# A Fourier mixing layer and a SoLU layer on one core: sorting the late units' transposed tokens by sign, and moving two products one step later

## The chip, the cores and the metric

The kernel runs on 1 core of one Trainium2 chip. The metric is the device time of one execution in microseconds (us), the median of several executions. The engines that matter here are TensorE (matrix products, "PE" in the profile, with its weight loads on a row of their own, "PEld"), VectorE ("DVE"), ScalarE ("ACT"), GpSimd ("POOL") and SyncE, which issues most DMAs ("SP"). Each engine works through its own instructions in program order and waits on the others through semaphores.

## The reference

```python
# x: (8, 3136, 256); w_in: (256, 1024); w_out: (1024, 256); g_ln: (1024,)
X = np.fft.fft(x, axis=1)
X = np.fft.fft(X, axis=2)
x = X.real.reshape(25088, 256)
h = x @ w_in
e = np.exp(h - max(h))                  # over the 1024 features of a token
solu = h * e / (sum(e) + 1e-9)
ln = (solu - mean(solu)) / sqrt(var(solu) + 1e-6) * g_ln
out = ln @ w_out                        # (25088, 256), float32
```

## The kernel before

The transform over the 3136 tokens of a sequence is split as 49 x 64. `transform1` makes the first part for a pair of sequences, chunk by chunk, and keeps it in DRAM (`zd`); `transform2` makes the second part for one frequency. The symmetry of a real input lets one result `q` serve two rows of the output, called the two signs; the transform over the features is folded into `w_in`. Four pairs of sequences give 100 units (25 of each pair), each of 128 tokens of either sign; the first unit of each pair (units 0, 25, 50, 75) has one sign only. A unit goes through `up` (the product with `w_in`), `even`, `join`, `expo`, `product`, `square` (SoLU and its statistics), is transposed by 32 x 32 blocks on VectorE (`turn_blocks`), has its blocks moved across partitions by DMA (`move_blocks`, once for two units, 16 DMAs), and four steps later meets `w_out`. There, odd units with both signs use the seven products of a Strassen-like scheme (`Down`, `sums`, `product7`), spread over an odd step and the following even one; the other units use two plain products (`down`), the first in an even step, the second (`plain`) in the following odd one.

In the transposed tile `uT` the tokens of the two signs alternate: the last index of `v` is the sign. The main loop works at step `i` on unit `i`, on the last products of unit `i - 4`, and on the first transform of the next pair (`ahead`, `ahead_pe`). `result(0)` is one PSUM bank, which `transform2`, `transform1` of the later pairs and the second plain product share.

```python
    qpool = ctx.enter_context(tc.tile_pool(name="qpool", bufs=4))
    ...
    def result(i):
        return ps_m.tile([P, 2 * D], FP32, tag=f"m{i % 4}", name="ps_m")
    ...
    def transform1(pr, s):
        ...
        ps = result(0 if pr.p else s).rearrange("p (l d) -> p l d", l=2)
        if s == NH // 2 - 1:
            parts = [(ps[0:ZR, 0], y[:, l], 0), (ps[0:ZR, 1], pr.y0[:, 0], 1), (ps[0:ZR, 1], y[:, l + 1], 2)]
        else:
            parts = [(ps[0:ZR], y[:, l : l + 2], 0)]
        pr.done.append(s)
        first = True
        for o, i, t in parts:
            for h, cs in enumerate((EVEN, ODD)):
                nc.tensor.matmul(o[..., cs], F[:, 2 * t + h, :], i[..., cs], start=first, stop=True,
                                 skip_group_check=True)
                first = False
        nc.scalar.copy(pr.z[:, l : l + 2, :], ps[0:ZR])
        if l == CH - 2:
            keep(pr, c, slice(0, ZR if pr.p else 4 * KG))
    ...
    def transform2(pr, k1):
        i, k = divmod(k1, KG)
        g = pr.g[i]
        table = T[0][:, :, k, :] if i == 0 else T[1][:, :, k1 - KG, :]
        ps = result(0)[:, 0 : KD * P]
        for h in range(KD):
            o = ps[:, h * P : (h + 1) * P].rearrange("p (b k) -> p b k", b=2)
            nc.tensor.matmul(o, g[:, k, h * P : (h + 1) * P], table,
                             start=(h == 0), stop=True, skip_group_check=True)
        return ps
    def take2(t, ps):
        t.q = qpool.tile([P, KD * P], FP32, tag="q", name="q")
        nc.scalar.copy(t.q, ps)
    def spread(t):
        t.r = small.tile([P, 1], FP32, tag="r", name="r")
        nc.sync.dma_start(out=t.r, in_=t.q[0:1, P : 2 * P])
    ...
    def up(t, c):
        ps = ps_h.tile([P, FF], FP32, tag=f"h{c}", name=f"ps_h{c}")
        for half in range(2):
            fs = slice(half * HW, (half + 1) * HW)
            nc.tensor.matmul(ps[:, fs], t.q[:, c * P : (c + 1) * P], Wi[:, c, fs], start=True, stop=True)
        return ps
    def even(t, ps):
        t.ev = fpool.tile([P, FF], FP32, tag="ev", name="ev", bufs=1)
        nc.vector.scalar_tensor_tensor(out=t.ev, in0=w_mid, scalar=t.r, in1=ps,
                                       op0=ALU.mult, op1=ALU.add)
    def join(t, s):
        if s == 0:
            t.nmax = small.tile([P, 2], FP32, tag="nmax", name="nmax")
        t.h[s] = fpool.tile([P, FF], FP32, tag="h", name="h", bufs=2)
        nc.vector.tensor_tensor_reduce(out=t.h[s], in0=t.h[0] if s else t.ev, in1=t.odd, scale=1.0 if s else -0.5,
                                       scalar=-3.0e38, op0=ALU.add, op1=ALU.max, accum_out=t.nmax[:, s : s + 1])
    ...
    class Batch:
        def __init__(self, by_blocks):
            if by_blocks:
                self.v = fpool.tile([P, 2, FF, 2], FP32, tag="v", name="v32", bufs=2)
            self.uT = fpool.tile([P, 2, KF, 4, 64], FP32, tag="uT", name="uT", bufs=2)
    def turn_blocks(t, s):
        for o in (s,) if len(t.signs) == 2 else (0, 1):
            nc.vector.transpose(out=t.batch.v[:, t.w, :, o], in_=t.u[s])
    ...
    def move_blocks(batch, units, engines=(nc.sync,)):
        v = batch.v[:, units].rearrange("p w (c q n) s -> p q (w c) (n s)", q=4, n=32)
        uT = batch.uT[:, units].rearrange("p w c i m -> p i (w c) m")
        for i in range(4):
            for q in range(4):
                a, b = slice(32 * i, 32 * i + 32), slice(32 * q, 32 * q + 32)
                engines[i % len(engines)].dma_start(out=uT[b, i], in_=v[a, q])
    ...
    def blocks(t):
        uT = t.batch.uT[:, t.w].rearrange("p c i (n s) -> p s c (i n)", s=2)
        return [uT[:, s, c : c + KF // 2] for s in range(2) for c in (0, KF // 2)]
    def sums(t):
        A11, A12, A21, A22 = blocks(t)
        t.S = spool.tile([P, 4, KF // 2, P], FP32, tag="S", name="S")
        for j, (a, b, op) in enumerate(((A21, A22, ALU.add), (t.S[:, 0], A11, ALU.subtract),
                                        (A11, A21, ALU.subtract), (A12, t.S[:, 1], ALU.subtract))):
            nc.gpsimd.tensor_tensor(out=t.S[:, j], in0=a, in1=b, op=op)
    def product7(o, a, b, start=False):
        n = KF // 2
        for c in range(n):
            nc.tensor.matmul(o, a[:, c], b[:, c], start=start and c == 0, stop=c == n - 1, skip_group_check=True)
    ...
    # class Down: seven products of a unit with both signs; the four quarters of the result are sums of them
        def p1(self):
            product7(self.C11, self.A11, Wo[:, 0 : KF // 2, 0:P], True)
        def seed(self):
            nc.scalar.copy(self.X, self.C11)
        def p4(self):
            product7(self.P53, self.A22, Ws[:, 3], True)
        def keep4(self):
            self.keep(1, 0, self.P53)
        def p2(self):
            product7(self.C11, self.A12, Wo[:, KF // 2 :, 0:P])
        def keep11(self):
            self.keep(0, 0, self.C11)
        def p5(self):
            product7(self.P53, self.t.S[:, 0], Ws[:, 0], True)
        def p6(self):
            product7(self.X, self.t.S[:, 1], Ws[:, 1])
        def p3(self):
            product7(self.P53, self.t.S[:, 3], Wo[:, KF // 2 :, P:])
        def p7(self):
            product7(self.X, self.t.S[:, 2], Ws[:, 2])
    ...
    def down(t, s, ps=None):
        uT = t.batch.uT[:, t.w].rearrange("p c i (n s) -> p c (i n) s", s=2)
        if ps is None:
            ps = (result(0) if s else bank(0))[:, 0:D]
        for c in range(KF):
            nc.tensor.matmul(ps, uT[:, c, :, s], Wo[:, c, :], start=(c == 0), stop=(c == KF - 1))
        return ps
    ...
    SUMS = [None] + [[f + 2 * c for c in range(NC)] for f in (3, 27, 51)]
    ...
    def ahead_pe(pr, i, half):
        for c in range(NC):
            if i == SUMS[pr.p][c] + 3:
                transform1(pr, c * CH // 2 + half)
    ...
        for i in range(whole + 1, len(units) + lag + 3):
            cur = units[i] if i < len(units) else None
            old = units[i - lag] if i < len(units) + lag else None
            seven = old and by_seven(i - lag)
            plain, late, scaled = late, None, []
            kept = units[i - lag - 3] if i > whole + 2 else None
            if seven:
                sums(old)
            if fresh:
                power(fresh)
            fresh = cur
            if kept:
                for s in kept.signs:
                    store(kept, s)
            if done:
                done.finish()
                done = None
            if cur:
                enter(i)
                even(cur, up(cur, 0))
                cur.odd = up(cur, 1)
                second_transform(i + 2)
                for s in cur.signs:
                    join(cur, s)
            if seven:
                new = Down(old, i == whole + 1)
                new.p1()
                new.seed()
            if half:
                half.p5()
                half.keep5()
                half.p6()
            if cur:
                expo(cur, 0)
            if half:
                half.keep6()
            if cur:
                if 1 in cur.signs:
                    expo(cur, 1)
                other_pairs(i, ahead_pe, 0)
            if plain:
                ps_o = down(*plain)
                if not cur:
                    scale(*plain, ps_o)
                    plain = None
            if seven:
                new.p4()
                new.p2()
            elif old is units[-1]:
                for s in (1, 0):
                    scaled.append((old, s, down(old, s, bank(2 * s)[:, 0:D])))
            elif old:
                scaled.append((old, 0, down(old, 0)))
                late = (old, 1) if 1 in old.signs else None
            if half:
                half.p3()
                half.p7()
                half, done = None, half
            if cur:
                for s in cur.signs:
                    product(cur, s)
                square(cur, 0)
            if plain:
                scale(*plain, ps_o)
            if seven:
                new.keep4()
                new.keep11()
                half = new
            if cur:
                if 1 in cur.signs:
                    square(cur, 1)
                other_pairs(i, ahead_pe, 1)
                for s in cur.signs:
                    turn_blocks(cur, s)
                if i >= len(units) - 2:
                    move_blocks(batches[-1], slice(cur.w, cur.w + 1), (nc.sync, nc.gpsimd) if cur.w else (nc.sync,))
                elif cur.w:
                    move_blocks(batches[-1], slice(0, 2))
                stats(cur)
            for t, s, ps_o in scaled:
                scale(t, s, ps_o)
            if cur:
                if cur.p == 0 and i in (5, 8, 11):
                    turn(first, (i + 1) // 3)
                for pr in pairs[1:]:
                    turn_parts(pr, i - pr.p * NK)
                other_pairs(i, ahead)
```

Of the kernel before, what the change touches and what calls it, by code (L numbers as in the profile page):

```python
# [9 lines left out]
FP32 = mybir.dt.float32  # L10
# [7 lines left out]
P = 128  # L18
# [3 lines left out]
NK = N1 // 2 + 1  # L22
# [13 lines left out]
def kernel(  # L36
# [19 lines left out]
    nc = tc.nc  # L56
    B, S, D = x.shape
    FF = moe_w_in.shape[1]
    KF = FF // P
# [9 lines left out]
    xpool = ctx.enter_context(tc.tile_pool(name="xpool", bufs=2))  # L69
    zpool = ctx.enter_context(tc.tile_pool(name="zpool", bufs=2))  # L70
    gpool = ctx.enter_context(tc.tile_pool(name="gpool", bufs=3))
    qpool = ctx.enter_context(tc.tile_pool(name="qpool", bufs=4))
    small = ctx.enter_context(tc.tile_pool(name="small", bufs=7))
    dram = ctx.enter_context(tc.tile_pool(name="dram", bufs=2, space=bass.MemoryType.DRAM))
    ps_h = ctx.enter_context(tc.tile_pool(name="ps_h", bufs=1, space=PSUM))
    fpool = ctx.enter_context(tc.tile_pool(name="fpool", bufs=2))
# [7 lines left out]
    Wo = const.tile([P, KF, D], FP32, name="Wo")  # L84
# [10 lines left out]
    def result(i):  # L95

        return ps_m.tile([P, 2 * D], FP32, tag=f"m{i % 4}", name="ps_m")
# [3 lines left out]
    class Pair:  # L101
        def __init__(self, p):
            self.p = p
            self.raw, self.y, self.y0 = {}, {}, None
            self.g, self.zs, self.done = {}, {}, []
# [26 lines left out]
    def add_mirror(pr, c, engine):  # L132

        xa, xb, _ = pr.raw[c]
        n = CH - 1 if c == NC - 1 else CH
        a, rb = xa[:, 0:n, :], xb[:, ::-1, :][:, 0:n, :]
        engine.tensor_tensor(out=a[:, :, 1:D], in0=a[:, :, 1:D], in1=rb[:, :, D - 1 : 0 : -1], op=ALU.add)
        engine.tensor_tensor(out=a[:, :, 0:1], in0=a[:, :, 0:1], in1=rb[:, :, 0:1], op=ALU.add)

    def fold(pr, c):  # L140

        xa, _, x0 = pr.raw.pop(c)
        y = xpool.tile([PR, CH, D], FP32, tag="y", name="y")
        copy = nc.scalar.copy if pr.p else nc.vector.tensor_copy
        fold_features(y, xa, copy)
        pr.y[c] = y
        if c == NC - 1:
            pr.y0 = xpool.tile([PR, 1, D], FP32, tag="y0", name="y0", bufs=1)
            fold_features(pr.y0, x0, copy)
# [143 lines left out]
    class Batch:  # L293


        def __init__(self, by_blocks):
            if by_blocks:
                self.v = fpool.tile([P, 2, FF, 2], FP32, tag="v", name="v32", bufs=2)
            self.uT = fpool.tile([P, 2, KF, 4, 64], FP32, tag="uT", name="uT", bufs=2)

    def turn_blocks(t, s):

        for o in (s,) if len(t.signs) == 2 else (0, 1):
            nc.vector.transpose(out=t.batch.v[:, t.w, :, o], in_=t.u[s])  # L304

    def turn_whole(t):

# [14 lines left out]

    def move_blocks(batch, units, engines=(nc.sync,)):

        v = batch.v[:, units].rearrange("p w (c q n) s -> p q (w c) (n s)", q=4, n=32)
        uT = batch.uT[:, units].rearrange("p w c i m -> p i (w c) m")
        for i in range(4):
            for q in range(4):
                a, b = slice(32 * i, 32 * i + 32), slice(32 * q, 32 * q + 32)
                engines[i % len(engines)].dma_start(out=uT[b, i], in_=v[a, q])  # L330
# [11 lines left out]
            nc.gpsimd.tensor_tensor(out=Ws[:, j], in0=a, in1=b, op=ALU.subtract)  # L342

    def blocks(t):
        uT = t.batch.uT[:, t.w].rearrange("p c i (n s) -> p s c (i n)", s=2)
        return [uT[:, s, c : c + KF // 2] for s in range(2) for c in (0, KF // 2)]

    def sums(t):
# [14 lines left out]
    def bank(i):  # L363

        if not banks:
            banks.extend(result(j) for j in (2, 3, 1))
        return banks[i]
# [68 lines left out]

    def down(t, s, ps=None):

        uT = t.batch.uT[:, t.w].rearrange("p c i (n s) -> p c (i n) s", s=2)
        if ps is None:  # L440
            ps = (result(0) if s else bank(0))[:, 0:D]
        for c in range(KF):
            nc.tensor.matmul(ps, uT[:, c, :, s], Wo[:, c, :], start=(c == 0), stop=(c == KF - 1))  # L443
        return ps

    def scale(t, s, ps):
# [167 lines left out]

    SUMS = [None] + [[f + 2 * c for c in range(NC)] for f in (3, 27, 51)]

    def ahead(pr, i):

        if i == (pr.p - 1) * NK:
            load(pr, 0)  # L620
            load(pr, 1)
        for c in range(NC):
            if i == SUMS[pr.p][c]:
                add_mirror(pr, c, nc.gpsimd)
            if i == SUMS[pr.p][c] + 1:
                fold(pr, c)
                if c + 2 < NC:
                    load(pr, c + 2)

    def ahead_pe(pr, i, half):  # L630

        for c in range(NC):
            if i == SUMS[pr.p][c] + 3:
                transform1(pr, c * CH // 2 + half)

    def turn_parts(pr, step):
# [5 lines left out]
    with tc.manual_schedule():  # L642
# [71 lines left out]
        units = [Unit(p, k1) for p in range(NP) for k1 in range(NK)]  # L714
# [5 lines left out]
            keep(first, c, slice(4 * KG, ZR))  # L720
        weights.load_table(1)
        lag = 4
        whole = 4

        def second_transform(i):
            if i < len(units):
                t = units[i]
                take2(t, transform2(pairs[t.p], t.k1))
                spread(t)

        def enter(i):
            cur = units[i]
            if i % 2 == 0:
                batches.append(Batch(i >= whole))
            cur.batch, cur.w = batches[-1], i % 2

        def begin(i):
# [12 lines left out]
        batches = []  # L750
# [50 lines left out]
# [19 lines that stand above are left out]
                enter(i)  # L820
                even(cur, up(cur, 0))
                cur.odd = up(cur, 1)
                second_transform(i + 2)
                for s in cur.signs:
                    join(cur, s)
            if seven:
# [62 lines that stand above are left out]
# [76 lines left out]
```

## Time and profile before

The median of 3 executions is 1176.87 us (1176.32 to 1179.43); the profiled execution spans 1174.4 us.

| Engine | busy us | share of the span | instructions |
|---|---|---|---|
| TensorE, products | 1132.6 | 96% | 5850 |
| VectorE | 1005.7 | 86% | 1376 |
| ScalarE | 762.4 | 65% | 1841 |
| GpSimd | 598.2 | 51% | 558 |

| Group of instructions | count | mean us |
|---|---|---|
| weights `uT` of the seven products (`Wo,uT`), load | 752 | 0.196 |
| weights `S` of the seven products (`Ws,S`), load | 1128 | 0.192 |
| block transpose 128 x 1024 on VectorE | 192 | 1.226 |
| copy of the first transform's result to SBUF on ScalarE, 100 x 512 | 54 | 0.574 |
| the DMA that moves blocks, 128 KB each | 752 | - |

A float32 product of one tile appears as two matmul instructions in the profile. Their durations overlap, since products are pipelined: the distance between the starts of two groups in the timeline says what a product really takes. A wait in the timeline stands in square brackets behind the group that waited, with what ended it.

### The profile page before, as it was taken

The numbers are of one execution on the slowest core, as the hardware profiler recorded it, in microseconds if no ns is written. First come the engines' busy times: TensorE is split into PE (matmuls) and PEld (weight loads), VectorE is DVE, ScalarE is ACT, GpSimd is POOL, SyncE is SP. The second block draws the span as 40 slices with busy tenths as digits, with TensorE's granted clock in tenths as the row PEclk, the third lists the DMA queues.
The fourth block names the chain that finished last, engine by engine and source line by source line (L and its number), as shares of the span: only waits on it lengthen the run. The fifth ranks groups of instructions, "written<-read, shape, count | busy, mean of one in ns | idle before, by whom it ended". The sixth has DMA issues, their size and how long they took to land. (4 is left out here: it accounts for less than half of the span.)

```text
span 1174.4 us, 18577 instructions
## 1 busy us (share of the span) xinstructions
PE 1132.6 (96%) x5850; PEld 881.2 (75%) x5850; DVE 1005.7 (86%) x1376; ACT 762.4 (65%) x1841; POOL 598.2 (51%) x558
## 2 busy tenths in 40 slices
PE   2988999999999999999999999999999999999997
PEld 1556787777877787877877777778777787778787
DVE  7789999998878999998879999999887898888870
ACT  4577666757756766767656666676666676677651
POOL 3036666563465566563556666554544334433444
PEclk9999999999999999999999999999999999999999
DMA  9672998865988998865879898865775565745553
GB/s 243 196 186 71 180 183 180 176 141 127 180 185 167 182 167 186 176 141 135 176 146 188 176 188 183 172 146 133 153 154 135 135 152 125 154 108 137 130 116 109
DMA packets 458465, 185.55 MB, mean 158 GB/s; under 512 B 425750, under 2 KB 440350, under 8 KB 458368
## 3 DMA queue, kind: packets, MB, share of 16 engines
q1 hardware_dynamic: 444608, 146.22, 60.4%
q0 software_dynamic: 13760, 38.16, 12.4%
q8 instruction: 47, 0.77, 0.3%
q14 instruction: 50, 0.41, 0.1%
HBM read 44.78 MB, written 38.80 MB: 71 GB/s over the span
## 5 line engine op out<-in xcount | busy, mean ns | idle before, releaser
L443 PE MATMUL ps_m<-Wo,uT 128*128 128x256 f32 x1632 | 369.2, 380 | 3.1 <-ACT uT L321 2.1
L238 PE MATMUL ps_h<-Wi,q 128*128 128x512 f32 x800 | 360.8, 593 | 3.0 <-DVE nmax L252 2.1
L443 PEld LDWEIGHTS ps_m<-Wo,uT 128*128 128x128 f32 x1632 | 314.2, 196 | 33.8 <-ACT uT L321 2.4
L268 DVE SCALAR_TENSOR_TENSOR u<-h,u 128x1024 f32<-128x1024 f32 x196 | 266.1, 1366 | 50.5 <-ACT u L261 36.1
L238 PEld LDWEIGHTS ps_h<-Wi,q 128*128 128x128 f32 x800 | 145.9, 190 | 149.9 <-issue 140.0
L275 ACT ACTIVATE h<-u,usum 128x1024 f32<-128x1024 f32 x196 | 224.4, 1145 | 34.3 <-DVE u L268 33.0
L354 POOL TENSOR_TENSOR S<-uT 128x512 f32<-128x512 f32 x94 | 130.4, 1387 | 208.5 <-issue 138.7
L261 ACT ACTIVATE u<-h,neg 128x1024 f32<-128x1024 f32 x196 | 225.3, 1150 | 6.4
L304 DVE STREAM_TRANSPOSE v<-u 128x1024 f32<-128x1024 f32 x192 | 227.8, 1226 | 0.1
L291 POOL TENSOR_TENSOR rs<-v,neg_half 128x2 f32<-128x2 f32 (+1 forms) x100 | 71.7, 717 | 251.8 <-ACT v L284 251.7
L252 DVE CUSTOM_DVE_ANT_0 h<-ev,ps_h 128x1024 f32<-128x1024 f32 x100 | 122.2, 1222 | 33.3 <-PE ps_h L238 23.5
L244 DVE SCALAR_TENSOR_TENSOR ev<-w_mid,r,ps_h 128x1024 f32<-128x1024 f32 x100 | 126.7, 1267 | 25.6 <-PE ps_h L238 20.6
L359 PE MATMUL ps_m<-Ws,S 128*128 128x128 f32 x1128 | 141.5, 275 | 1.8 <-ACT ot L390 1.8
L216 ACT COPY q<-ps_m 128x256 f32<-128x256 f32 x100 | 36.8, 368 | 159.4 <-PE ps_m L210 155.9
L359 PEld LDWEIGHTS ps_m<-Ws,S 128*128 128x128 f32 x1128 | 133.6, 192 | 2.7 <-issue 1.6
L252 DVE CUSTOM_DVE_ANT_0 h<-h,ps_h 128x1024 f32<-128x1024 f32 x96 | 117.3, 1221 | 13.8
L454 POOL DMA_INDIRECT out_dram<-ot,idx x96 | 100.8, 1050 | 30.7 <-issue 18.7
L359 PE MATMUL ps_m<-Wo,uT 128*128 128x128 f32 x752 | 104.2, 282 | 0.1
L182 PE MATMUL ps_m<-y,F 98*100 98x258 f32 (+3 forms) x288 | 73.4, 390 | 24.7 <-DVE y L130 21.8
L210 PEld LDWEIGHTS ps_m<-T,g 128*128 128x128 f32 x400 | 60.2, 191 | 49.1 <-issue 41.7
L359 PEld LDWEIGHTS ps_m<-Wo,uT 128*128 128x128 f32 x752 | 96.1, 196 | 0.9 <-issue 0.5
L259 ACT ACTIVATE neg<-nmax 128x1 f32<-128x1 f32 x196 | 38.4, 196 | 81.5 <-DVE nmax L252 73.6
(87 smaller groups left out, 1186.7 us busy)
## 6 DMA issues: line engine op xcount, KB each, us to landing
uT<-v SPq DMA_DIRECT2D x752, 128.0 KB
out_dram<-ot SPq DMA_DIRECT2D x100, 128.0 KB
g<-zd POOLq DMA_DIRECT2D x72, 160.0 KB, 5.6
xa<-in_x_dram SPq DMA_DIRECT2D x28, 392.0 KB
zd<-z SPq DMA_DIRECT2D x24, 400.0 KB
raw_in<-in_moe_w_in_dram SPq DMA_DIRECT2D x4, 512.0 KB
raw_out<-in_moe_w_out_dram SPq DMA_DIRECT2D x2, 1024.0 KB
r<-q SPq DMA_DIRECT2D x100, 0.5 KB
```

The lines of the kernel that those rows point to most:

```text
L182: nc.tensor.matmul(o[..., cs], F[:, 2 * t + h, :], i[..., cs], start=first, stop=True, skip_group_check=True)
L238: nc.tensor.matmul(ps[:, fs], t.q[:, c * P : (c + 1) * P], Wi[:, c, fs], start=True, stop=True)
L244: nc.vector.scalar_tensor_tensor(out=t.ev, in0=w_mid, scalar=t.r, in1=ps, op0=ALU.mult, op1=ALU.add)
L252: nc.vector.tensor_tensor_reduce(out=t.h[s], in0=t.h[0] if s else t.ev, in1=t.odd, scale=1.0 if s else -0.5, scalar=-3.0e38, op0=ALU.add, ...
L261: nc.scalar.activation(out=t.u[s], in_=t.h[s], func=ACT.Exp, bias=t.neg[:, s : s + 1], accum_out=t.esum[:, s : s + 1])
L268: nc.vector.scalar_tensor_tensor(out=t.u[s], in0=t.h[s], scalar=1.0, in1=t.u[s], op0=ALU.mult, op1=ALU.mult, accum_out=t.usum[:, s : s + 1])
L275: nc.scalar.activation(out=t.h[s], in_=t.u[s], func=ACT.Square, bias=t.usum[:, s : s + 1], scale=-float(FF), accum_out=t.ssq[:, s : s + 1])
L304: nc.vector.transpose(out=t.batch.v[:, t.w, :, o], in_=t.u[s])
L354: nc.gpsimd.tensor_tensor(out=t.S[:, j], in0=a, in1=b, op=op)
L359: nc.tensor.matmul(o, a[:, c], b[:, c], start=start and c == 0, stop=c == n - 1, skip_group_check=True)
L443: nc.tensor.matmul(ps, uT[:, c, :, s], Wo[:, c, :], start=(c == 0), stop=(c == KF - 1))
L454: dma = nc.gpsimd.indirect_dma_start(out=out, out_offset=bass.IndirectOffsetOnAxis(ap=idx[:, i : i + 1], axis=0), in_=t.ot[s], in_offset=None)
```

## The change

From unit 66 on, the transposed tiles `v` and `uT` hold all tokens of the first sign together and then all of the second, so that the weights of the last products are read from consecutive addresses instead of every second one. The DMAs that move the blocks then move runs of 32 elements where they moved runs of 64. From there on the second transform is made three units ahead instead of two, so that `r`, the small DMA that it starts, has one more step; the pool of `q` gets a fifth buffer. Apart from that, the two products (`transform1`) that pair 3 had at step 54 move to step 55, in which, as unit 50 has one sign only, no plain product stands.

```diff
--- before.py
+++ after.py
@@ -69,7 +69,7 @@
     xpool = ctx.enter_context(tc.tile_pool(name="xpool", bufs=2))
     zpool = ctx.enter_context(tc.tile_pool(name="zpool", bufs=2))
     gpool = ctx.enter_context(tc.tile_pool(name="gpool", bufs=3))
-    qpool = ctx.enter_context(tc.tile_pool(name="qpool", bufs=4))
+    qpool = ctx.enter_context(tc.tile_pool(name="qpool", bufs=5))
     small = ctx.enter_context(tc.tile_pool(name="small", bufs=7))
     dram = ctx.enter_context(tc.tile_pool(name="dram", bufs=2, space=bass.MemoryType.DRAM))
     ps_h = ctx.enter_context(tc.tile_pool(name="ps_h", bufs=1, space=PSUM))
@@ -293,15 +293,27 @@
     class Batch:
 
 
-        def __init__(self, by_blocks):
+
+
+        def __init__(self, by_blocks, apart):
+            self.apart = apart
             if by_blocks:
-                self.v = fpool.tile([P, 2, FF, 2], FP32, tag="v", name="v32", bufs=2)
-            self.uT = fpool.tile([P, 2, KF, 4, 64], FP32, tag="uT", name="uT", bufs=2)
+                self.v = fpool.tile([P, 2, KF, 2, P] if apart else [P, 2, FF, 2], FP32, tag="v", name="v32", bufs=2)
+            self.uT = fpool.tile([P, 2, KF, 2, P] if apart else [P, 2, KF, 4, 64], FP32, tag="uT", name="uT", bufs=2)
+
+        def of(self, w):
+
+            if self.apart:
+                return self.uT[:, w].rearrange("p c s k -> p s c k")
+            return self.uT[:, w].rearrange("p c i (n s) -> p s c (i n)", s=2)
 
     def turn_blocks(t, s):
 
         for o in (s,) if len(t.signs) == 2 else (0, 1):
-            nc.vector.transpose(out=t.batch.v[:, t.w, :, o], in_=t.u[s])
+            if t.batch.apart:
+                nc.vector.transpose(out=t.batch.v[:, t.w, :, o, :], in_=t.u[s].rearrange("p (c k) -> p c k", c=KF))
+            else:
+                nc.vector.transpose(out=t.batch.v[:, t.w, :, o], in_=t.u[s])
 
     def turn_whole(t):
 
@@ -322,8 +334,13 @@
 
     def move_blocks(batch, units, engines=(nc.sync,)):
 
-        v = batch.v[:, units].rearrange("p w (c q n) s -> p q (w c) (n s)", q=4, n=32)
-        uT = batch.uT[:, units].rearrange("p w c i m -> p i (w c) m")
+        v, uT = batch.v[:, units], batch.uT[:, units]
+        if batch.apart:
+            v = v.rearrange("p w c s (q n) -> p q (w c s) n", q=4)
+            uT = uT.rearrange("p w c s (i n) -> p i (w c s) n", i=4)
+        else:
+            v = v.rearrange("p w (c q n) s -> p q (w c) (n s)", q=4, n=32)
+            uT = uT.rearrange("p w c i m -> p i (w c) m")
         for i in range(4):
             for q in range(4):
                 a, b = slice(32 * i, 32 * i + 32), slice(32 * q, 32 * q + 32)
@@ -342,7 +359,7 @@
             nc.gpsimd.tensor_tensor(out=Ws[:, j], in0=a, in1=b, op=ALU.subtract)
 
     def blocks(t):
-        uT = t.batch.uT[:, t.w].rearrange("p c i (n s) -> p s c (i n)", s=2)
+        uT = t.batch.of(t.w)
         return [uT[:, s, c : c + KF // 2] for s in range(2) for c in (0, KF // 2)]
 
     def sums(t):
@@ -436,11 +453,11 @@
 
     def down(t, s, ps=None):
 
-        uT = t.batch.uT[:, t.w].rearrange("p c i (n s) -> p c (i n) s", s=2)
+        uT = t.batch.of(t.w)
         if ps is None:
             ps = (result(0) if s else bank(0))[:, 0:D]
         for c in range(KF):
-            nc.tensor.matmul(ps, uT[:, c, :, s], Wo[:, c, :], start=(c == 0), stop=(c == KF - 1))
+            nc.tensor.matmul(ps, uT[:, s, c], Wo[:, c, :], start=(c == 0), stop=(c == KF - 1))
         return ps
 
     def scale(t, s, ps):
@@ -613,6 +630,9 @@
 
 
     SUMS = [None] + [[f + 2 * c for c in range(NC)] for f in (3, 27, 51)]
+
+
+    SHORT = 2 * NK + 5
 
     def ahead(pr, i):
 
@@ -630,7 +650,8 @@
     def ahead_pe(pr, i, half):
 
         for c in range(NC):
-            if i == SUMS[pr.p][c] + 3:
+            due = SUMS[pr.p][c] + 3
+            if i == due + (due == SHORT - 1):
                 transform1(pr, c * CH // 2 + half)
 
     def turn_parts(pr, step):
@@ -720,6 +741,8 @@
             keep(first, c, slice(4 * KG, ZR))
         weights.load_table(1)
         lag = 4
+
+        far = 65
         whole = 4
 
         def second_transform(i):
@@ -731,7 +754,7 @@
         def enter(i):
             cur = units[i]
             if i % 2 == 0:
-                batches.append(Batch(i >= whole))
+                batches.append(Batch(i >= whole, i > far))
             cur.batch, cur.w = batches[-1], i % 2
 
         def begin(i):
@@ -820,7 +843,9 @@
                 enter(i)
                 even(cur, up(cur, 0))
                 cur.odd = up(cur, 1)
-                second_transform(i + 2)
+
+                for j in range(2 + (i > far), 3 + (i >= far)):
+                    second_transform(i + j)
                 for s in cur.signs:
                     join(cur, s)
             if seven:
```

## Prediction

> **What bounds the kernel now.** I read the page's 40 slices first, then the waits, then TensorE's timeline, because the share of busy time says nothing of single gaps.
>
> ```profile
> PE   2988999999999999999999999999999999999997
> DMA  9672998865988998865879898865775565745553
> ```
>
> From the third slice on TensorE never drops under 80% (and the page's row of its clock shows 9 throughout), and the DMA engines are less loaded in the last third (5 to 7 tenths) than in the middle (8 to 9). The waits of TensorE from 790 us to the end are one line: the engine, what waited, for what, us, times, longest.
>
> ```profile
> PE ps_m L443 <- ACT q L216: 0.5, 1, 0.5
> ```
>
> So in the region where the layout changes, time is what TensorE's own instructions take. Shortening a wait of another engine there gives nothing; shortening a TensorE instruction gives its whole length. What they take I read from the distances of starts in the timeline (start, us, instructions):
>
> ```profile
> 1090.16 3.63 PE L443 MATMUL ps_m<-Wo,uT 128*128 128x256 f32 x16
> 1093.62 1.10 PE L359 MATMUL ps_m<-Ws,uT 128*128 128x128 f32 x8
> 1094.56 1.11 PE L359 MATMUL ps_m<-Wo,uT 128*128 128x128 f32 x8
> ...
> 1099.38 1.95 PE L359 MATMUL ps_m<-Ws,S 128*128 128x128 f32 x16
> 1101.16 3.62 PE L443 MATMUL ps_m<-Wo,uT 128*128 128x256 f32 x16
> ```
>
> Eight products with weights from `uT` (every second address) take 1094.56 - 1093.62 = 0.94 us, 117 ns each; sixteen with weights from `S` (consecutive) take 1.78 us, 111 ns each. The plain product, 256 columns wide, takes 3.46 / 16 = 216 ns with `uT` as weights; a load of 196 ns that overlaps is hidden there.
>
> The other place is the short step, 55:
>
> ```profile
> 653.18 3.60 PE L238 MATMUL ps_h<-Wi,q 128*128 128x512 f32 x8
> ...
> 659.89 1.88 PE L238 MATMUL ps_h<-Wi,q 128*128 128x512 f32 x4
> 662.34 1.96 PE L238 MATMUL ps_h<-Wi,q 128*128 128x512 f32 x4 [0.57 <-DVE nmax L252]
> 664.13 0.61 PE L210 MATMUL ps_m<-T,g 128*128 128x128 f32 x4
> 665.72 2.02 PE L359 MATMUL ps_m<-Ws,S 128*128 128x128 f32 x16 [0.98 <-ACT ot L390]
> 667.97 1.11 PE L182 MATMUL ps_m<-y,F 98*100 98x258 f32 x4 [0.23 <-ACT q L216]
> ```
>
> TensorE idles 0.57 + 0.98 + 0.23 = 1.78 us here. It has overtaken VectorE, whose work runs without a wait for TensorE from 628 to 690 us in its own timeline, and which reaches the `even` of step 55 only at 658.15 us. ScalarE follows VectorE:
>
> ```profile
> 650.89 0.56 ACT L185 COPY z<-ps_m 100x512 f32<-100x512 f32 x1
> ...
> 663.52 0.19 ACT L261 ACTIVATION_READ_ACCUMULATOR u<-h,neg 128x1 f32 x1
> ```
>
> The first line is the copy of a first-transform product in step 54; the other is the end of the second exponential of step 55, at 663.7 us.
>
> **What the Trainium skill says.** "TensorE: Matmul & The Clock Gate", section "LDWEIGHTS (loading the stationary operand)", lets the time of a weight load depend on the columns alone; nothing there speaks of the step between them. The trace differs a little: 196 against 192 ns in the records, 117 against 111 ns in the distances. "DMA: Bandwidth & Descriptors", section "Why small descriptors are slow (HBM only)", spares transfers between places in SBUF the penalty, and gives each packet a fixed cost of about 3 cycles beside one per 32 bytes: 11 cycles for 256 bytes, so by my estimate 7 for 128, and 14 / 11 = 1.27 times the time for the same bytes. This case's trace shows a fixed part too (below). "Perfetto Trace Analysis", section "Optimizing Tensor Performance", wants independent groups of products in different PSUM banks so that the copy of one overlaps the next. `transform1` does not do that here: both halves and `transform2` share one bank, and where products follow `transform2` directly in that bank the trace shows a wait of 0.46 us for the copy of `q` (368.68 and 380.20 us).
>
> **Part 1, the layout.** Removed: the step of two addresses in the weights of p1, p2 and p4, 24 instructions in an odd unit. Each group of eight takes 0.94 us now and should take 1.78 / 2 = 0.89 us: 3 x 0.05 = 0.15 us per odd unit. The odd units from 67 to 97 are 16 (99 is not done by seven): 16 x 0.15 = 2.4 us, all on the path. The plain products stay as they are, since their 216 ns are set by the columns. The block transposes on VectorE (1.226 us) and the sums on GpSimd may change by a few ns, off the path.
>
> Added: twice the packets. A move of 128 KB has 512 packets of 256 bytes, then 1024 of 128. Packets and their share of 16 engines' time, of the SyncE queue, in a 0.6 us stretch with `r` alone (4 bytes each), and in an 8 us stretch of moves:
>
> ```profile
> q1 hardware_dynamic: 145, 0.00, 11.9%
> ```
> ```profile
> q1 hardware_dynamic: 1088, 0.26, 14.7%
> ```
>
> That is 0.119 x 0.6 x 16 / 145 = 7.9 ns for 4 bytes and 0.147 x 8 x 16 / 1088 = 17.3 ns for about 256. Between them, 128 bytes should take 12.5 ns, so 25 for what took 17.3: 1.45 times. The queue that issues them:
>
> ```profile
> 1097.07 12.86 SPq L330 DMA_DIRECT2D uT<-v  x16
> ...
> 1118.14 12.95 SPq L330 DMA_DIRECT2D uT<-v  x16
> ```
>
> It needs 12.86 us for the moves of two units, 0.80 each, and 3.4 us for two stores and two `r`, in a period of 21.07 us. The first moves of a burst are issued in 0.65 us; moves of half the size in the tail take 0.59 to 0.65. Issue depends little on size, and the DMA share in this burst is about 0.72 where other bursts reach 1.39. So I take 0.9 to 1.1 us per move afterwards, 14 to 18 us for sixteen. The limit is (21.07 - 3.4) / 16 = 1.10 us. Below it nothing shows; the even unit's tile would land some 3 us later, of about 7 us in hand (moves issued by 861.5 us, landed some 2 us later, its plain product about 871 us). I expect 0 us here, with little room.
>
> **Part 2, three ahead.** `r` stands behind the moves in the queue; issued at 862.34 us it is needed by VectorE about 867 us, so slower moves would make it late. One step more removes that danger, and gains nothing by itself. At step 65 two second transforms follow each other in one bank: the 0.46 us seen above, once.
>
> **Part 3, the short step.** Removed from step 54: two products of about 0.87 us (four instructions each, starts 0.86 to 0.94 us apart), 1.73 us. Added to step 55, the same. If they just filled the 1.78 us of idle time, the gain would be 1.7 us. I do not believe it, and this is my main choice. In step 55 TensorE's order becomes: up, second transform, p1, first half, p4, p2, second half, then up of step 56. The second half needs the bank of the first, so the copy of the first half, which ScalarE has in its order behind the second exponential: 663.6 us, done about 664.15. In step 54 a plain product of 3.46 us stood between the halves; here only p4 and p2, 1.9 us, so TensorE comes to the second half about 659 to 660 us and waits some 4 to 5 us. VectorE and so the exponential cannot come earlier, as VectorE had no wait for TensorE before. Then: second half 664.25 to 665.1, up of step 56 to 668.55 (3.44), second transform to 669.0, the S products to 670.8 (1.78), next first-transform half to 671.65, where the plain product starts. It started at 668.91. The waits of 0.98 and 0.23 us have then disappeared into the longer one: the plain product comes 2.7 us later, not 1.7 earlier. TensorE is saturated from there on, so 2.7 us reach the end, less perhaps 0.3 that a 0.34 us gap at 736.96 us can swallow.
>
> **Sum.** 1176.87 - 2.4 + 0.46 + 2.7 - 0.3 = 1177.3 us; with a little for the DMA risk, 1177.5.
>
> **Rivals.** (a) The moved products fill the idle time as meant, if VectorE too gets through step 54 sooner: 1176.87 - 2.4 + 0.5 - 1.7 = 1173.3 us. For it: the idle time has nearly the right size. Against it: VectorE's unbroken row and the order on ScalarE. (b) The moves become the bound: if a packet of 128 bytes took as long as one of 256, sixteen moves would take 25.7 us, the period 29.1 instead of 21.07, and 16 periods would give 128 us, less 7 in hand: some 1290 us. At 1.2 us per move it is 1.6 us a period, about 20 us in all: 1197. For it: moves already slow from 0.65 to 0.80 us within a burst. Against it: 7.9 ns for a 4-byte packet. (c) The weight load does not depend on the step, and 117 ns have another cause: 1180 with my part 3.
>
> **Range and chances.** My part 3 has about 60%, the rival (a) 30%; the moves stay hidden with about 80%, cost 1 to 20 us with 13%, more with 7%. That gives 1173 to 1186 us as the range. Two per cent are 23.5 us: faster 0.01, the same 0.91, slower 0.08.
>
> **What would show it.** In the new trace: groups of eight `Wo,uT` and `Ws,uT` 0.89 us apart in late steps; TensorE's first late wait still under 1 us; a wait of the products with `F` on ScalarE's copy of `z` of 4 to 5 us about 660 us (right), or a stretch without gaps about 655 to 669 us (rival a); sixteen moves in 14 to 18 us. Waits of TensorE or GpSimd on the DMA of `uT` would make it wrong, upwards; so would plain products under 216 ns, downwards.

## The result and the profile after

The changed kernel takes 1183.3 us (median of 6, 1181.2 to 1184.99), beside 1177.98 us for the kernel before on the same chip: 1.0046 times as long, 95% interval 1.0027 to 1.0065. In a second comparison with more executions (e9 below) the ratio was 1.0026 (1.0019 to 1.0034). It is slower, by 3 to 5 us, and inside the predicted range.

The rows of the page that answer to those shown of before, and its main DMA queue:

```profile
PE   2888999999999999999999899999999999999997
DMA  9772998865987998865879898867999997989984
...
q1 hardware_dynamic: 581824, 146.22, 69.7%
```

From the 28th slice on, where the new layout has begun, the DMA engines are at 7 to 9 tenths (but for the last slice) instead of 4 to 7. The queue carries the same 146.22 MB in 581824 packets instead of 444608, and takes 69.7% of 16 engines' time instead of 60.4%. TensorE's row has a new 8 in its 23rd slice, which holds the short step.

The waits of TensorE after 600 us (engine, what waited, for what; us, times, longest):

```profile
PE ps_m L182 <- ACT z L185: 4.3, 1, 4.3
PE ps_m L376 <- POOL S L371: 1.9, 1, 1.9
...
```

Two waits are new: one for the copy of `z` in the short step, and one in the tail, at the S products of step 102. The lines left out are four of 0.5 us or less, none of them for `uT` or `r`. For the wait in the tail the profile names GpSimd's sums. But its first product needs only the first of these, and the bank that it writes comes free when ScalarE has scaled the result of p4, and ScalarE itself waited for a store:

```profile
1158.71 0.63 ACT L407 ACTIVATE ot<-ps_m,rs 128x128 f32<-128x128 f32 x2 [2.62 <-DMA out_dram<-ot,idx]
```

TensorE goes on at 1159.22 us, just behind the first of these two scalings (in the trace of e9 the profile names this scaling itself).

TensorE in the steps 54 to 56 (start, us, instructions, and in brackets the wait):

```profile
655.80 3.60 PE L238 MATMUL ps_h<-Wi,q 128*128 128x512 f32 x8
...
660.62 1.03 PE L182 MATMUL ps_m<-y,F 98*100 98x258 f32 x4
661.97 1.21 PE L376 MATMUL ps_m<-Ws,uT 128*128 128x128 f32 x8 [0.32 <-DVE ot L411]
663.01 1.10 PE L376 MATMUL ps_m<-Wo,uT 128*128 128x128 f32 x8
668.43 1.58 PE L182 MATMUL ps_m<-y,F 98*100 98x258 f32 x4 [4.31 <-ACT z L185]
669.80 4.86 PE L238 MATMUL ps_h<-Wi,q 128*128 128x512 f32 x8
674.50 0.61 PE L210 MATMUL ps_m<-T,g 128*128 128x128 f32 x4
...
677.59 3.62 PE L460 MATMUL ps_m<-Wo,uT 128*128 128x256 f32 x16
```

and ScalarE just before 668.43 us:

```profile
666.66 1.15 ACT L261 ACTIVATE u<-h,neg 128x1024 f32<-128x1024 f32 x1
667.72 0.19 ACT L261 ACTIVATION_READ_ACCUMULATOR u<-h,neg 128x1 f32 x1
667.81 0.56 ACT L185 COPY z<-ps_m 100x512 f32<-100x512 f32 x1
```

This is the predicted order: the first half runs at 660.62 us, its copy stands behind the second exponential, and the second half waits 4.31 us for it. This execution is 4.22 us behind the profile of before already when step 54 begins; without that the second half would start at 664.21 us, and 664.25 was predicted. Then comes what was not predicted: the second half takes 669.80 - 668.43 = 1.37 us instead of 0.86, and `up` of step 56 takes 4.70 us instead of 3.44. The stretches of the trace say why (stretch, its length, busy us and instructions of TensorE's products, of its loads, VectorE, ScalarE, GpSimd, then the granted clock as a share of full speed, DMA share, GB/s):

```profile
664.00:668.00 4.00, 0.12 (x2) 0.00 (x0) 3.69 (x5) 2.88 (x7) 3.97 (x3) 1.00 0.96 180
668.00:670.00 2.00, 1.57 (x5) 1.25 (x6) 2.00 (x5) 2.00 (x6) 0.29 (x1) 0.73 0.69 200
670.00:672.00 2.00, 2.00 (x4) 0.81 (x3) 1.67 (x2) 1.97 (x6) 0.00 (x0) 0.50 0.19 50
672.00:674.00 2.00, 2.00 (x5) 0.76 (x4) 1.02 (x1) 0.34 (x2) 1.39 (x2) 0.92 0.50 120
```

After the wait TensorE's clock is granted at 0.73, 0.50 and 0.92. From the `up` of step 54 (644.60 us here, 640.38 before) to the plain product of step 56 it is 32.99 us instead of 28.53: 4.46 us more, of which the slow clock is 0.51 + 1.26 = 1.77. Below, "the stretch" is this one.

A late odd step, with the new layout:

```profile
1117.59 1.05 PE L376 MATMUL ps_m<-Wo,uT 128*128 128x128 f32 x8
1118.48 3.62 PE L460 MATMUL ps_m<-Wo,uT 128*128 128x256 f32 x16
1121.94 1.05 PE L376 MATMUL ps_m<-Ws,uT 128*128 128x128 f32 x8
1122.83 1.06 PE L376 MATMUL ps_m<-Wo,uT 128*128 128x128 f32 x8
1123.72 3.60 PE L238 MATMUL ps_h<-Wi,q 128*128 128x512 f32 x8
```

Each group of eight takes 0.89 us (it was 0.94), the plain product 3.46 us as before. The SyncE queue in the same region:

```profile
1063.08 16.07 SPq L347 DMA_DIRECT2D uT<-v  x16
...
1083.99 14.78 SPq L347 DMA_DIRECT2D uT<-v  x16
```

Sixteen moves take some 15 to 16 us, and 18.9, 19.7 and 20.2 in three bursts that have loads of `g` beside them; before it was 13 to 15.5.

### The profile page after: what moved, and what is told of

It is laid out like the page before. It is cut to its first block, busy times and chain, and to the rows that moved or that the text cites. A ratio compares the mean times of both kernels' runs of the same rounds, so it can differ in the third digit from the quotient of the medians.

```text
span 1182.9 us, 18577 instructions
## 1 busy us (share of the span) xinstructions
PE 1135.8 (96%) x5850; PEld 878.5 (74%) x5850; DVE 1007.7 (85%) x1376; ACT 762.6 (64%) x1841; POOL 598.6 (51%) x558
## 3 DMA queue, kind: packets, MB, share of 16 engines
q1 hardware_dynamic: 581824, 146.22, 69.7%
## 5 line engine op out<-in xcount | busy, mean ns | idle before, releaser
L316 DVE STREAM_TRANSPOSE v<-u 128x1024 f32<-128x1024 f32 x124 | 147.2, 1226 | 0.1
L407 ACT ACTIVATE ot<-ps_m,rs 128x128 f32<-128x128 f32 x188 | 64.9, 359 | 31.9 <-PE ps_m L376 23.1
```

## The experiments

Theory A: the short step costs, through ScalarE's order and the slow clock after the wait; the layout gains on TensorE. Theory B: the doubled packets cost, and the short step is harmless. All ratios below are to the kernel before, measured on the same chip; e1 to e4, e5 to e8 and e9 to e12 were measured together, with 1177.64, 1178.12 and 1177.61 us for the kernel before. (The times are medians; the ratios are estimates of their own, and can differ in the last digit from the quotient of two medians.)

| run | what it is | us | ratio (95% interval) |
|---|---|---|---|
| e1 | changed, short-step move undone | 1176.37 | 0.9988 (0.9981 to 0.9995) |
| e2 | before, short-step move alone | 1182.24 | 1.0040 (1.0029 to 1.0051) |
| e3 | changed, first copy ahead of the exponentials | 1179.05 | 1.0011 (1.0000 to 1.0021) |
| e4 | e1, last two units in the old layout | 1175.74 | 0.9984 (0.9977 to 0.9991) |
| e5 | e4, second transform two ahead | 1179.67 | 1.0010 (0.9999 to 1.0021) |
| e6 | e4, from unit 32 on | 1195.98 | 1.0155 (1.0128 to 1.0182) |
| e7 | before, three ahead alone | 1178.74 | 1.0001 (0.9992 to 1.0010) |
| e8 | e4, products in step 55, both copies ahead | 1175.45 | 0.9980 (0.9970 to 0.9991) |
| e9 | the changed kernel again | 1180.59 | 1.0026 (1.0019 to 1.0034) |
| e10 | e8, stores one step earlier | 1172.49 | 0.9963 (0.9950 to 0.9977) |
| e11 | before, stores one step earlier | 1173.93 | 0.9973 (0.9963 to 0.9983) |
| e12 | e1, stores one step earlier | 1175.72 | 0.9988 (0.9977 to 0.9999) |

**The move undone, and the move alone (e1, e2).**

```diff
-            if i == due + (due == SHORT - 1):
+            if i == due:
```

> The changed kernel with the two products back at step 54; layout and three-ahead stay. Theory A (the short step costs: TensorE waits 4.3 us for the copy of z and then runs below its full clock for some us): this run is about 4.5 us faster than the changed kernel, so 1177 to 1180 us, no wait of TensorE on z over 1 us, and about 28.5 us from the up of step 54 to the plain product of step 56 as in the kernel before (33.0 in the changed one). Theory B (the doubled packets of the moves cost, and the short step is harmless or gains): it stays at 1183 us or gets slower by up to 1.7 us.

The time fell to 1176.37 us, a little below the kernel before; the stretch was 669.85 - 641.32 = 28.53 us and TensorE did not wait for `z`. For the move alone, the kernel before got that one condition:

> The kernel before with nothing but the two products moved to step 55. Theory A: slower than before by 4 to 5 us, with the wait of about 4.3 us on the copy of z and a clock share under 1 in the 3 us after it. Theory B: the 1.8 us of idle time are filled, 1.0 to 1.7 us faster than before.

It took 1182.24 us, 4.6 us more than before. Its trace has the same wait, 4.30 us, and a longer slow time:

```profile
664.00:668.00 4.00, 0.99 (x3) 0.84 0.80 164
668.00:670.00 2.00, 2.00 (x5) 0.50 0.48 164
670.00:672.00 2.00, 2.00 (x3) 0.50 0.35 74
672.00:674.00 2.00, 2.00 (x4) 0.60 0.74 219
```

(stretch, length, busy TensorE, clock, DMA share, GB/s). Here the clock stays low until about 673 us, and the stretch is 34.19 us. Theory B falls: the move costs by itself, and without it the layout gains.

**The first copy moved forward (e3).** In step 55 alone:

```diff
             if cur:
+                if i == SHORT:
+                    other_pairs(i, ahead_pe, 0)
                 expo(cur, 0)
```

(and the later call skips that step).

> The changed kernel, but in step 55 the first of the moved products and its copy are issued ahead of the two exponentials, so that the copy no longer stands behind them on ScalarE. Theory A: the 4.3 us wait is gone and so is the slow clock; the time is that of the run without the move (about 1178 us), not less, since VectorE is behind in this stretch and TensorE then waits for it about 1.8 us as before. Rival (the products fill the idle time once the copy is out of the way): 1.5 us less than the run without the move. If the wait has another cause than ScalarE's order, it stays and the time is 1183 us.

The wait of the second half is gone, but the time is 2.7 us above e1, not equal to it. TensorE's row shows where the wait went:

```profile
662.48 3.61 PE L238 MATMUL ps_h<-Wi,q 128*128 128x512 f32 x8
669.34 1.22 PE L210 MATMUL ps_m<-T,g 128*128 128x128 f32 x4 [3.25 <-ACT z L185]
670.35 3.01 PE L376 MATMUL ps_m<-Ws,S 128*128 128x128 f32 x16
```

The copy of the second half still stands behind the second `square`, and the next second transform needs the same bank: it waits 3.25 us, and runs at a slow clock after it (2.84 us for sixteen products instead of 1.78). The expectation missed, and the cause is confirmed, since the wait followed the copy that was left behind: ScalarE's order has two such places, and I had cleared one.

**Both copies moved forward (e8).** In step 55 both halves and both copies come ahead of the exponentials, the second after p4:

```diff
                 new.p1()
+                if i == SHORT:
+                    other_pairs(i, ahead_pe, 0)
                 new.seed()
+                if i == SHORT:
+                    new.p4()
+                    other_pairs(i, ahead_pe, 1)
```

(and the later calls skip that step).

> As the run with the old layout for the last two units, with the two products at step 55, but both of them and both copies are issued ahead of the exponentials of that step. Theory A (VectorE is behind in this stretch, so TensorE waits the same 1.8 us wherever the products stand): no wait on z over 1 us, no slow clock, about 28.5 us from the up of step 54 to the plain product of step 56, and the time of the run without the move (1175 to 1177 us). Rival (the idle time is filled once no copy is in the way): 27 us for that stretch and 1.5 us less in all.

```profile
659.17 1.03 PE L182 MATMUL ps_m<-y,F 98*100 98x258 f32 x4
...
664.43 0.61 PE L210 MATMUL ps_m<-T,g 128*128 128x128 f32 x4
666.08 2.02 PE L376 MATMUL ps_m<-Ws,S 128*128 128x128 f32 x16 [1.04 <-ACT ot L407]
668.33 1.11 PE L182 MATMUL ps_m<-y,F 98*100 98x258 f32 x4 [0.23 <-ACT q L216]
669.27 3.62 PE L460 MATMUL ps_m<-Wo,uT 128*128 128x256 f32 x16
```

No wait for `z`, and the stretch (from 641.14 us) is 28.13 us, 0.4 us under that of the kernel before; the time, 1175.45 us, cannot be told from e4's. So even with no copy in the way, 1.73 us of products put into 1.78 us of idle time bring next to nothing: the waits of 1.04 and 0.23 us at the end of the step stay. That they follow VectorE's pace through ScalarE, so that TensorE meets them wherever its own work stands, fits VectorE's row, which waits for TensorE nowhere near, but no run makes VectorE faster here.

**The last two units (e4).**

```diff
-                batches.append(Batch(i >= whole, i > far))
+                batches.append(Batch(i >= whole, far < i < len(units) - 2))
```

> As the run without the short-step move, but the last two units (98, 99) keep the old layout. Theory A: the tail (from p1 of step 101 to the end) goes back from 31.8 to about 30.5 us, the wait of 1.9 us at the S products of step 102 is gone; 1 to 1.5 us faster than the run without the move, about 1 to 2 us faster than the kernel before. If the tail's wait does not come from the moves of the last units, the time stays that of the run without the move.

TensorE's tail, from p1 of step 101 to its last three plain products, falls from 15.18 us (e1) to 13.19 (13.32 before), and its wait there is gone. But the time is only 0.6 us less than e1's, and the intervals overlap: the tail's wait is undone, its price in time is not shown. GpSimd's row suggests why, here of e1, with the last stores of the second sign:

```profile
1156.30 0.96 POOL L471 DMA_INDIRECT out_dram<-ot,idx  x1 [2.48 <-issue]
1159.67 0.96 POOL L471 DMA_INDIRECT out_dram<-ot,idx  x1 [2.41 <-DMA out_dram<-ot,idx]
1162.99 0.96 POOL L471 DMA_INDIRECT out_dram<-ot,idx  x1 [2.36 <-issue]
1166.14 0.96 POOL L471 DMA_INDIRECT out_dram<-ot,idx  x1 [2.19 <-ACT ot L465]
1169.31 0.96 POOL L471 DMA_INDIRECT out_dram<-ot,idx  x1 [2.20 <-issue]
```

In the program each of these stores waits until the one before it has landed, and they follow each other 3.15 to 3.4 us apart. The last one is issued at 1169.31 us in e1 and at 1169.45 in e4, though TensorE starts its last products 2.6 us earlier in e4.

**Two ahead (e5).** The loop of the change goes back to `second_transform(i + 2)`.

> As the run with the old layout for the last two units (no short-step move), but the second transform stays two ahead in all steps. Theory: r is issued about 17 us after a burst of moves begins (21 us in the few bursts that share the engines with loads of g) and is needed about 21 us after, so it is in time nearly always; VectorE waits for r under 5 us in total, the 0.46 us at step 65 is saved, and the time is within 1 us of that run (1175 to 1177 us). Rival (three ahead is what makes the layout bearable): VectorE waits for r in each second step, 1180 us or more.

A miss. VectorE's waits in its trace:

```profile
DVE ev L244 <- DMA r<-q: 18.9, 7, 4.4
```

18.9 us in seven steps, and 1179.67 us, 3 to 4 us more than e4 by the ratios or the times. The bursts of moves are long enough to bring `r` late, and VectorE makes up most of the delay but not all: TensorE takes 461.4 us from the plain product of step 56 to the `up` of step 99, against 456.6 in e4. Three ahead belongs to the layout; without it the layout brings no gain.

**Three ahead alone (e7).** Only that loop and the fifth buffer, in the kernel before.

> The kernel before with nothing but the second transform three ahead from step 66 and the fifth buffer of q. Theory: one wait of TensorE of about 0.5 us on the copy of q at step 65, otherwise nothing: 0 to 1 us slower than before. If the addresses that the fifth buffer shifts or the earlier use of g matter, more than 1 us either way.

1178.74 us, no difference that can be measured; the trace has the predicted wait of 0.5 us of the second transform on the copy of `q`. With the weight loads' gain of 2.4 us and this wait, e4 should be 1.9 us below the kernel before, and it is 1.9 below (1.1 to 2.7 by its interval).

**From unit 32 (e6).** `far = 31`.

> As the run with the old layout for the last two units, but the new layout and three ahead begin at unit 32 instead of 66. Theory (weight loads): 17 more odd units at 0.15 us give 2.5 us, if the DMA holds; sixteen moves should take 15 to 22 us there, so a wait or two of TensorE may cost up to 2 us: 1173 to 1176 us. Rival (the DMA engines are full in the middle of the kernel and the restriction to late units is needed): TensorE waits on uT, r or g, 1180 us or more.

1195.98 us: the rival was right, and my 2.5 us for weight loads drown. TensorE's waits between 350 us and the end begin so:

```profile
PE ps_m L460 <- DMA out_dram<-ot: 6.0, 2, 3.4
PE ps_m L460 <- DMA r<-q: 3.5, 2, 2.6
PE ps_m L460 <- DMA xa<-in_x_dram: 3.3, 1, 3.3
...
PE ps_m L460 <- DMA uT<-v: 1.0, 1, 1.0
```

All of them are plain products that wait for their `uT`. The releaser named is whatever DMA came last; the product needs all its moves, and each of the four longest waits ends 3.4 to 4.0 us after the last move of a burst of more than 21 us. Bursts take up to 23.1 us there, and ten of the fifteen that begin between 424 and 761 us are above the 17.7 us that fit into a period.

**Again, and the end of the kernel (e9 to e12).** In e10 to e12 each unit is stored one step earlier, behind the sums that it needs (the loop ends one step earlier too):

```diff
-            kept = units[i - lag - 3] if i > whole + 2 else None
+            kept = units[i - lag - 2] if i > whole + 1 else None
             ...
-            if kept:
-                ...
             if done:
                 done.finish()
                 done = None
+            if kept:
+                ...
```

> The changed kernel itself once more, beside the other runs on one chip. If the parts add up (short step +4.7 us, layout and three ahead together -1.4 us, by the runs of each), it is 3 to 4 us slower than the kernel before; if the tail's wait is followed by a slow clock in most executions, another 1 to 2 us come on top (5 to 5.5 us).

> The kernel before with nothing but the stores one step earlier. Theory (the chain of stores sets the end): 1.5 to 3 us faster than before. Rival: no difference.

> The changed kernel without the short-step move, new layout to the end, stores one step earlier. If the tail's wait of 1.8 us (on ScalarE's scaling for step 102) comes from a buffer of ot that a late store holds, the wait is gone here, although the moves of the last units keep their doubled packets; time 1172.5 to 1175 us. If it comes from GpSimd's own issue of those moves, the wait stays at over 1 us.

> The run with both copies ahead of the exponentials and the old layout for the last two units, and each unit stored one step earlier (right after its sums are finished). In the tail the stores of the second sign wait for each other, 3.16 us apiece, and end 4 to 6 us after TensorE. Theory (this chain sets the end): one store less stands in it, so 1.5 to 3 us less, 1172.5 to 1174.5 us. Rival (TensorE's end sets it, or an earlier store holds GpSimd up elsewhere): no gain, 1175 to 1177 us or more.

The changed kernel was 3.0 us slower this time, near the sum of its parts (e1 -1.3, e2 +4.6). Earlier stores alone bring the kernel before 3.2 to 3.7 us (e11), a little more than expected: the chain of stores, not TensorE, set its end. In e12 the wait on ScalarE's scaling in the tail is gone. So a buffer of `ot`, held by a late store, had caused it, as ScalarE's wait for a store in the first profile said; but a new wait shows behind it:

```profile
1148.86 1.99 PE L376 MATMUL ps_m<-Ws,S 128*128 128x128 f32 x16
1152.89 3.69 PE L460 MATMUL ps_m<-Wo,uT 128*128 128x256 f32 x16 [2.04 <-issue]
```

That product needs the tile of unit 98, whose sixteen moves are issued from 1135.66 to 1150.67 us, 15.0 us instead of 11.9 before. So e12 gained nothing over e1 (both 0.9988), and its expected time was missed: TensorE now ends last. In the last two units the new layout costs TensorE some 2 us and gains nothing: from the `up` of step 99 to the last products it takes 32.35 us in e12, 30.04 in e10, which keeps the old layout there, and 30.20 before. e10 combines the rest: 1172.49 us, below the kernel before and below the changed one. That it is also below e11 is not clear of noise.

## Why the prediction was right or wrong

**Part 1, the weight loads: right in rate.** 0.05 us per group of eight, as worked out; the plain products unchanged. By e4 and e7 it is worth about 2 us where the tail does not take it back. In the changed kernel part of it is lost there: the tail's wait (1.86 us in the first profile, 1.54 in the trace of e9) was not in the prediction, which looked at the landing of the tiles between steps but not at the last two units.

**The moves: right, with less room than it said.** "14 to 18 us for sixteen" was 15 to 16, with three bursts of up to 20.2. These three were over the limit of 17.7 us that was worked out from the queue, and TensorE still did not wait, so what was in hand could carry single long bursts; in e6, where two bursts in three passed the limit, the kernel lost 18 us. The 1.45 for the time of the packets was too low (the last section has the number).

**Part 2: the cost right, the need understated.** e7 shows the predicted near-nothing. The prediction had `r` in danger; before e5 I then talked myself out of it, and 18.9 us of waits answered.

**Part 3, the main choice: right in sign and mechanism, too small.** The wait was 4.31 us, of the predicted 4 to 5. The term that failed is "up of step 56 to 668.55 (3.44)", with the 0.86 of the second half before it: both took for granted that TensorE goes on at full speed after a wait. It did not: 2.7 us predicted for the plain product's delay, 4.46 measured in the trace, and the difference is the 1.77 us of slow clock. The credit of 0.3 us failed too: the gap that was to swallow it is still there, 0.35 us at 745.63. Rival (a), the filled idle time, was wrong even in its best form (e8).

**The sum.** The prediction had 0.6 us; measured were 3 to 5. Single profiles show where, if their stretches are compared and not their spans, since the executions differ from the start: the first `up` begins at 56.16 us in the profile of before, at 60.19 in the first profile after, and at 55.6 to 59.0 in the others.

| TensorE, us | before | after, first profile | after, e9 |
|---|---|---|---|
| `up` of step 54 to plain product of step 56 | 28.53 | 32.99 | 32.51 |
| from there to `up` of step 99 | 458.13 | 456.59 | 456.58 |
| from there to the last three plain products | 30.20 | 33.80 | 31.81 |

The first line has the predicted wait and 1.6 to 1.8 us of slow clock. The second is the layout's gain less the wait for `q`, 1.5 us. The third has the tail's wait, of which the end of the kernel feels a part. In the first profile it too was followed by a slow clock: the sixteen products of S and the plain product behind them took 2.42 and 4.56 us instead of 1.78 and 3.46; in the trace of e9 they did not. How often that happens was not measured, and why one comparison gave 5 us and the other 3 stays open.

That 1183.3 us lies in the range is partly luck. Its upper part was made for slow moves, and these cost TensorE nothing before the tail; the slow clock and the tail's wait, which came in their place, were not thought of. Two slips changed nothing: the sum of rival (b) gives some 1298 us, not 1290, and TensorE's row does drop under 80% once, in its last slice, the tail.

## What to carry to other kernels

Before work is moved into an engine's idle time, ask which engine made it idle, and in whose program order the moved work's result is taken out of its PSUM bank: here the copy stood behind work of the very engine that was late. A wait can cost more than its length: those of 3.3 and 4.3 us in the short step were followed by a slow clock that took another 1.6 to 3.3 us (e3, e9, e2 and the first profile). And a gain on TensorE reaches the end only if what follows it ends earlier too: here the chain of stores did not, until it was made shorter (e4, e11).

## What the runs showed of the hardware that was not expected

The clock after a wait: 4.31 us of waiting were followed by stretches granted 0.73, 0.50 and 0.92, 4.30 us in e2 by 0.50, 0.50 and 0.60. The Trainium skill, "TensorE: Matmul & The Clock Gate", section "Part 1: The HAM clock gate (the "warmup" mystery)", says that the clock halves after an idle window of about 3.4 us and that this window runs freely. The halving agrees. But in the tail of the changed kernel's first profile 1.86 us of waiting sufficed (0.86, 0.50 and 0.79 in the three stretches of 2 us from 1159 us), while 1.78 us in e1 was followed by products of the usual length. In e6 a wait of 2.63 us was followed by 0.71, 0.50 and 0.94, and one of 2.66 us by 1.00. So a wait shorter than the window can be enough, and its length alone does not decide; on what it depends stays open.

Eight products of 128 columns whose weights are read with a step of two addresses took 0.94 us, with consecutive addresses 0.89: 6 ns for each. The plain products, of 256 columns, took 3.46 us for sixteen with either.

Halving the length of the pieces that a DMA moves within SBUF, at the same bytes, made bursts about 1.2 times as long (15 to 16 us against 13). That is only the time in which the queue issues them. Over ten late bursts (908.5 to 1119 us before, 917.5 to 1127 after) the packets of that queue took 51.1% of 16 engines' time before and 83.6% after, 1.6 times as much, more than the 1.27 and the 1.45 of the prediction.
